# The last plain product of w_out by seven of its own, with one set of left sums and eight PSUM banks

## The chip, the cores and the metric

The kernel runs on one core of a Trainium2 chip. Times are microseconds on the device; lower is better. The core's engines are TensorE (PE: matmuls, and PEld: the loads of their stationary operand), VectorE (DVE), ScalarE (ACT), GpSimd (POOL) and SyncE (SP, which here only issues DMA). Each has its own queue of instructions and takes them in order; they meet at semaphores.

## The reference: what is computed

Normalised attention, and then a layer of two matmuls with silu between them; all in float32.

```python
q_n, k_n = rmsnorm(q, g_q), rmsnorm(k, g_k)            # q, k, v: (8, 12, 448, 64)
attn = softmax(q_n @ k_n.T / sqrt(64))
x = (attn @ v) as (3584, 768)                          # heads side by side
h = x @ w_in                                           # w_in: (768, 2048)
out = (h * sigmoid(h)) @ w_out                         # w_out: (2048, 768)
```

The change concerns the last line alone: a product of 3584x2048 by 2048x768.

## The kernel before

Attention for eight batches, `x @ w_in` and the silu come first; the silu's result goes to `hidden` in DRAM, transposed, so that rows of the 2048 lie on the partitions. They end near 904 us. The rest of the time is the second matmul, and all that follows here is about it.

**Quads.** The 3584 rows of the output are cut into 7 quads of 512. `quad(q)` computes one: a left operand of 512x2048 (from `hidden`) by the right operand `w_out`, 2048x768, which stays in SBUF. Each quad cuts both operands into 2x2 halves and forms the result from 7 products of sums of halves, in place of 8 (Strassen's scheme in Winograd's form). The products are numbered 1 to 7 and come in the order 4, 1, 2, 5, 6, 7, 3. Each is 256x1024 by 1024x384. The left sums of this outer level are four steps, `sum_left(0)` to `sum_left(3)`, each two VectorE operations of 1024 columns. They overwrite the halves in place, between the products that still need the old and those that need the new contents.

**Two ways to make a product.** `single` (L1063) does it plainly: for each of two tiles of 128 rows, 8 matmuls of 384 columns into one PSUM bank. A float32 matmul is two records in the trace, so a plain product is 32 records. `deep` (L1027) applies the scheme of seven once more inside the product: 7 small products of 4 matmuls of 192 columns, 56 records, in the order 1, 2, 6, 5, 3, 7, 4. Small product 1 takes a11, 2 takes a12, 4 takes a22, all raw quarters of the left operand; 6 takes the left sum s2, 5 takes s1, 3 takes s4, 7 takes s3. `sum_deep_left(name)` makes these four sums on VectorE, 512 columns each, in places `deep_lefts`; there are two sets of them, taken in turn by the products in `DEEP`. The sums of the right operand, `sum_deep_right(name)`, are made once, in the first quad, and kept for all quads in `deep_rights`: 16 VectorE operations of 192 columns for each product. One of every four overwrites part of w_out's half (b12), which the plain form of that same product still reads; so it comes after it.

**Evictions.** Each small product's bank is read once: 1 and 5 by a ScalarE copy (L1047, L1051) to p1 and p5, the others by a VectorE addition (`plus`, L704) that combines them. A product that adds to what is already in its result (`more`) has four additional additions of 192 columns. After product 7, eight VectorE operations of 384 columns combine the outer results, and `save_out` stores them.

**Which is deep.** Product 1 (`SINGLE`) is plain in every quad; its result goes to two places by ScalarE. In the first quad products 4, 2, 5 and 6 are plain too, since their right sums are made then, and 7 and 3 are deep. In the other quads all but 1 are deep.

**Order.** Everything is written out by hand in the order of issue. The left sums of a product are issued one or two products ahead of it, behind the evictions of an earlier product and ahead of those of the one before it. `fetch` (L966) loads the next quad's halves of the left operand, 1 MB each, from `hidden` as soon as the old contents have been used; it and most stores wait in SyncE's one queue.

**Banks.** PSUM has eight banks. Here two belong to the pool `ps_mm` (used by `single`) and six to `ps_alone` (used by `deep`). `bank(n)` (L726), which takes three of four tiles from `ps_alone` and one from `ps_mm` in turn, serves only the matmul before, `x @ w_in`.

Of the kernel before, what the change touches and what calls it, by code (L numbers as in the profile page):

```python
# [11 lines left out]
F32 = mybir.dt.float32  # L12
# [15 lines left out]
BANK = 512  # L28
# [152 lines left out]
def kernel(  # L181
# [25 lines left out]
    nc = tc.nc  # L207
# [75 lines left out]

    room = Room(nc, const, w_in, z)
    rms = [const.tile([P, 32], F32, name=f"rms{i}") for i in range(2)]
    spare = const.tile([P, 2 * J * D], F32, name="squares")
    minus_half = const.tile([P, 1], F32, name="minus_half")
    ident = const.tile([P, P], F32, name="ident")
    ones = const.tile([P, 3, D // 2], F32, name="ones")
# [4 lines left out]
    norm = Norm(nc, z, rms, minus_half)  # L294

    first_q = room.rest[:, ds(7 * nq, nq)]
    first_squares = [spare, room.rest[:, ds(6 * nq, nq // 2)]]
    g1, both = (
        room.rest[0:1, ds(room.rest.shape[1] - (i + 1) * 2 * D, 2 * D)].rearrange(
            "p (two d) -> p two d", two=2  # L300
# [156 lines left out]
def bounded(  # L457
# [41 lines left out]
    rows_q = [place["q0"], extra[:, 0:nq]]  # L499
    raw_q = [extra[:, ds(nq, nq)], extra[:, ds(2 * nq, nq)]]  # L500
    other = extra[:, ds(3 * nq, 4 * S)].rearrange("p (i h s) -> p i h s", i=2, h=2)
    scratch = [spare, extra[:, ds(3 * nq + 4 * S, nq // 2)]]


    n = 2 * room.COLS
# [194 lines left out]
    def minus(a, b, out):  # L700
        nc.vector.tensor_tensor(out=out, in0=a, in1=b, op=ALU.subtract)

    def plus(a, b, out):
        nc.vector.tensor_tensor(out=out, in0=a, in1=b, op=ALU.add)  # L704
# [11 lines left out]
    def right_sums(b11, b12, b21, b22, t1, t2, t4):  # L716

        minus(b12, b11, t1)
        minus(b22, t1, t2)
        minus(b22, b12, b12)  # L720
        minus(b21, t2, t4)
# [4 lines left out]
    def bank(n):  # L726
        turn = turns["next"] = (turns["next"] + 1) % 4
        if ps_alone is None or turn == 0:
            return ps_mm.tile([P, BANK], F32, name="mm")[:, 0:n]
        return ps_alone.tile([P, BANK], F32, name="alone")[:, 0:n]  # L730
# [210 lines left out]
    def take(n, *which):  # L941

        for i in which or range(len(regions)):
            a, at = regions[i]
            if at + n <= a.shape[1]:
                regions[i][1] += n
                return a[:, ds(at, n)]
        raise AssertionError

    SINGLE = 1  # L950
    DEEP = (4, 2, 5, 6, 7, 3)
    size = HF * 2 * P
    left = {at: take(size, 0) for at in ((1, 1), (0, 0), (0, 1))}
    left[1, 0] = take(size, 1)

    deep_lefts = [[take(size // 4, 8, 7, 6) for _ in range(4)] for _ in range(2)]
    results = {(1, 1): [take(z.HALF, i) for i in (7, 5)]}
    copies = [take(QUARTER, i) for i in (0, 0, 1, 2)]
    for at in ((1, 2), (2, 1), (2, 2)):
        a = take(2 * z.HALF)  # L960
        results[at] = [a[:, ts(t, z.HALF)] for t in range(2)]
    a = take(2 * z.HALF)
    aside = [a[:, ts(t, z.HALF)] for t in range(2)]
    deep_rights = {name: [take(4 * QUARTER) for _ in range(3)] for name in DEEP}

    def fetch(q, i, r):  # L966

        if q >= QUADS:
            return
        dst = left[i, r].rearrange("p (f c) -> p f c", f=HF)  # L970
        source = hidden.rearrange("(f r) p c -> r p f c", r=2)
        nc.sync.dma_start(dst, source[r, :, :, ds((4 * q + 2 * i) * P, 2 * P)])
# [7 lines left out]
    def sum_left(step):  # L980
        a11, a12, a21, a22 = (
            left[at].rearrange("p (n c) -> p n c", n=2) for at in ((0, 0), (0, 1), (1, 0), (1, 1))
        )
        for n in range(2):
            left_sums(a11[:, n], a12[:, n], a21[:, n], a22[:, n], a22[:, n], a11[:, n], a12[:, n], (step,))
# [5 lines left out]
    def deep_left(name):  # L991

        a = LEFTS[name].rearrange("p (i m t c) -> p m t i c", i=4, m=2, t=2)
        sums = [
            x.rearrange("p (i c) -> p i c", i=4) for x in deep_lefts[DEEP.index(name) % 2]
        ]
        return [a[:, 0, 0], a[:, 1, 0], a[:, 0, 1], a[:, 1, 1]] + sums

    def sum_deep_left(name):
        a11, a12, a21, a22, s1, s2, s3, s4 = deep_left(name)  # L1000
        plus(a21, a22, s1)
        minus(s1, a11, s2)
        minus(a11, a21, s3)
        minus(a12, s2, s4)

    def deep_right(name, i):
        b = right_one(name, i)
        h = [ts(k, QUARTER) for k in range(2)]
        return [b[:, 0, h[0]], b[:, 0, h[1]], b[:, 1, h[0]], b[:, 1, h[1]]] + [
            x[:, ts(i, QUARTER)] for x in deep_rights[name]  # L1010
        ]

    def sum_deep_right(name):

        for i in ORDER:
            right_sums(*deep_right(name, i))

    def of_seven(name, a, b):

# [4 lines left out]
            5: (s1, t1), 6: (s2, t2), 7: (s3, b12),  # L1024
        }[name]

    def deep(name, out, more, then=lambda t, h: None):  # L1027

        a = deep_left(name)
        out = [[x[:, ts(h, QUARTER)] for h in range(2)] for x in out]  # L1030
        p1, u2, u3, p5 = copies

        def product(of):
            t = ps_alone.tile([P, BANK], F32, name="alone")[:, 0:QUARTER]
            for i in ORDER:
                x, y = of_seven(of, a, deep_right(name, i))
                nc.tensor.matmul(t, x[:, i], y, start=i == ORDER[0], stop=i == ORDER[-1])  # L1037
            return t

        def added(x, o):  # L1040

            if not more:
                return x
            plus(o, x, o)
            return o

        nc.scalar.copy(p1, product(1))  # L1047
        plus(product(2), added(p1, out[0][0]), out[0][0])
        then(0, 0)
        plus(product(6), p1, u2)  # L1050
        nc.scalar.copy(p5, product(5))  # L1051
        plus(u2, p5, u3)
        x = added(u3, out[0][1])
        plus(product(3), x, out[0][1])
        then(0, 1)
        plus(product(7), u2, u3)
        x = added(u3, out[1][0])
        plus(product(4), x, out[1][0])
        plus(u3, added(p5, out[1][1]), out[1][1])
        then(1, 0)  # L1060
        then(1, 1)

    def single(name, t):  # L1063

        a = LEFTS[name].rearrange("p (f t c) -> p f t c", f=HF, t=2)
        o = ps_mm.tile([P, BANK], F32, name="mm")[:, 0 : z.HALF]
        steps = [(i, m) for i in ORDER for m in range(2)]
        for n, (i, m) in enumerate(steps):
            nc.tensor.matmul(  # L1069
                o, a[:, 2 * i + m, t], right_one(name, i)[:, m],  # L1070
                start=n == 0, stop=n == len(steps) - 1,
            )
        return o

    def save_out(q, i, j):
        for t in range(2):
            store(
                nc, out, z, (4 * q + 2 * (i - 1) + t) * P, results[i, j][t], (j - 1) * z.HALF,
                nc.gpsimd if q == QUADS - 1 and i == 2 else nc.sync,
            )  # L1080

    def quad(q):
        c = results

        def product(name, out, more):
            if q > 0 or name in DEEP[4:]:
                deep(name, out, more)
                return
            for t in range(2):
                o = single(name, t)  # L1090
                if more:
                    plus(o, out[t], out[t])
                else:
                    nc.scalar.copy(out[t], o)
            sum_deep_right(name)

        if q == 0:
            fetch(0, 1, 0)
            sum_deep_right(7)
        product(4, c[2, 1], False)  # L1100
        sum_left(0)
        sum_left(2)
        if q == 0:
            sum_deep_right(3)
        else:
            sum_deep_left(2)
        for t in range(2):
            o = single(SINGLE, t)
            nc.scalar.copy(c[1, 1][t], o)
            nc.scalar.copy(c[1, 2][t], o)  # L1110
        sum_left(1)
        if q > 0:
            sum_deep_left(5)
        product(2, c[1, 1], True)
        save_out(q, 1, 1)
        sum_left(3)
        if q > 0:
            sum_deep_left(6)
        product(5, c[2, 2], False)
        fetch(q + 1, 1, 1)  # L1120
        sum_deep_left(7)
        product(6, c[1, 2], True)
        fetch(q + 1, 0, 0)
        sum_deep_left(3)
        product(7, aside, False)
        for t in range(2):
            plus(aside[t], c[1, 2][t], aside[t])
            plus(c[1, 2][t], c[2, 2][t], c[1, 2][t])
            plus(c[2, 2][t], aside[t], c[2, 2][t])
            plus(c[2, 1][t], aside[t], c[2, 1][t])  # L1130
        save_out(q, 2, 2)
        save_out(q, 2, 1)
        fetch(q + 1, 1, 0)
        if q == QUADS - 1:

            def then(t, h):
                store(
                    nc, out, z, (4 * q + t) * P, c[1, 2][t][:, ts(h, QUARTER)],
                    z.HALF + h * QUARTER, *((nc.scalar, nc.sync)[:: 1 if h else -1]),
                )  # L1140

            deep(3, c[1, 2], True, then)
            return
        sum_deep_left(4)
        product(3, c[1, 2], True)
        save_out(q, 1, 2)
        fetch(q + 1, 0, 1)
# [406 lines left out]
```

## Time and profile before

| | |
|---|---|
| time, median of 3 runs | 1371.86 us (1369.43 to 1373.31) |
| span of the profiled execution | 1369.6 us |
| second matmul (first to last TensorE record) | 903.7 to 1363.0 us |
| `deep`'s matmuls, L1037, busy | 346.94 us in 2128 records |
| `single`'s matmuls, L1069, busy | 114.66 us in 352 records |
| mean granted TensorE clock | 0.995 |

The page gives busy time by engine; a chain of waits follows the execution back from its last instruction; the windows give busy time by engine in a stretch; the timeline gives the instructions of a stretch in order, "x2" being two of a kind merged, with the idle time ahead of one and what ended it in brackets. A name such as `work`, `rows`, `x`, `sums_x`, `stage`, `parts`, `squares` or `W` in a line is the big SBUF tile in which a piece lies, since the second matmul reuses the first part's room; `mm` and `alone` are the two PSUM pools.

### The profile page before, as it was taken

To read this page: it belongs to the slowest core of one execution; us is meant where nothing else is said; L and a number is where in the kernel's file an instruction comes from. 1 tells how busy PE (TensorE), PEld (TensorE's weight loads), DVE (VectorE), ACT (ScalarE), POOL (GpSimd) and SP (SyncE) were. 2 spreads that over 40 slices of the span, in tenths; PEclk is the share of its full clock that TensorE was granted. 3 is DMA by queue.
4 is the path that set the end of the run, shared out by engine and by line. 5 is a ranking of instruction groups with operands and counts; after the bars stand their busy time and mean duration, and the time that the engine had idled before them with its cause. 6 is when DMAs were issued, how large, how long until landed. Compare 5 with 4: busy or idle time off the path is not lost.

```text
span 1369.6 us, 19386 instructions
## 1 busy us (share of the span) xinstructions
PE 1335.0 (97%) x7185; PEld 818.4 (60%) x7185; DVE 886.6 (65%) x1497; ACT 517.5 (38%) x882; POOL 342.5 (25%) x241
## 2 busy tenths in 40 slices
PE   7998999999999999999999999999999999999998
PEld 4333444444444444444444455556898989898987
DVE  3887867785644444744443586677877676777775
ACT  5875555655455545544644244320000010100000
POOL 4764444343332332233221044410000000000001
PEclk9999999999999999999999999999999999999999
DMA  7663445333223222322221257422323232322311
GB/s 176 190 160 101 111 133 152 93 103 80 78 74 96 78 73 77 104 78 78 78 79 37 99 167 252 157 96 64 105 74 97 73 97 79 97 91 85 113 58 38
DMA packets 175404, 139.40 MB, mean 102 GB/s; under 512 B 104036, under 2 KB 159268, under 8 KB 175300
## 3 DMA queue, kind: packets, MB, share of 16 engines
q1 hardware_dynamic: 174624, 137.08, 34.1%
q8 instruction: 59, 0.97, 0.3%
q0 software_dynamic: 352, 0.79, 0.2%
q14 instruction: 45, 0.37, 0.1%
q10 hardware_dynamic: 324, 0.20, 0.1%
HBM read 88.47 MB, written 41.29 MB: 95 GB/s over the span
## 4 chain that ended last, share of the span: by engine, by line
PE 90%; DVE 4%; ACT 2%; issue 2%; SPq 1%; DMA 1%; DVEq 0%; ACTq 0%
PE mm L745 28%; PE alone L1037 25%; PE av L611 9%; PE mm L1069 8%; PE sc L579 8%; PE alone L745 7%; PE sc L546 1%; PE sc L561 1%; PE sc L645 1%; DVE work L654 1%; PE mm L645 1%; ACT work L584 1%; DVE work L625 1%; DVE rms L396 1%; DMA hidden<-stage 0%
## 5 line engine op out<-in xcount | busy, mean ns | idle before, releaser
L745 PE MATMUL mm<-x,W 128*128 128x448 f32 x636 | 255.5, 546 | 5.2 <-DVE stage L704 2.7
L584 ACT ACTIVATE work<-sc,rms 128x448 f32<-128x448 f32 x324 | 184.1, 631 | 88.4 <-PE sc L579 74.9
L424 POOL TENSOR_TENSOR rms<-rms,minus_half 128x14 f32<-128x14 f32 (+4 forms) x55 | 138.5, 2520 | 251.8 <-DVE rms L420 199.9
L745 PEld LDWEIGHTS mm<-x,W 128*128 128x128 f32 x636 | 118.3, 191 | 127.7 <-issue 107.1
L745 PE MATMUL mm<-sums_x,W 128*128 128x448 f32 x456 | 183.0, 542 | 0.8 <-DVE parts L704 0.8
L579 PE MATMUL sc<-work 64*64 64x448 f32 x1344 | 165.0, 548 | 6.1 <-ACT work L584 4.0
L625 DVE TENSOR_TENSOR work<-work 128x896 f32<-128x896 f32 (+1 forms) x114 | 124.9, 1130 | 58.8 <-ACT work L584 56.6
L611 PE MATMUL av<-work,rows 64*64 64x448 f32 x1296 | 153.7, 548 | 7.8 <-issue 2.8
L745 PEld LDWEIGHTS mm<-sums_x,W 128*128 128x128 f32 x456 | 85.3, 190 | 86.5 <-issue 81.1
L451 POOL DMA_DIRECT2D out_dram<-x x4 | 2.2, 565 | 450.6 <-DVE x L704 450.6
L611 PEld LDWEIGHTS av<-work,rows 64*64 64x64 f32 x1296 | 51.9, 133 | 96.5 <-issue 86.8
L579 PEld LDWEIGHTS sc<-work 64*64 64x64 f32 x1344 | 52.2, 133 | 88.4 <-issue 34.7
L1037 PE MATMUL alone<-W,rows 128*128 128x192 f32 x552 | 103.1, 326 | 0.0
L396 DVE TENSOR_REDUCE rms<-squares 112x8 f32<-112x512 f32 (+1 forms) x80 | 52.4, 655 | 73.0 <-ACT squares L395 72.2
L1037 PEld LDWEIGHTS alone<-W,rows 128*128 128x128 f32 x552 | 92.0, 190 | 0.0
L1069 PE MATMUL mm<-W,work 128*128 128x384 f32 x264 | 88.7, 486 | 0.0
L1037 PE MATMUL alone<-W,work 128*128 128x192 f32 x468 | 88.1, 326 | 0.0
L760 POOL TENSOR_TENSOR parts<-parts,stage 128x448 f32<-128x448 f32 x31 | 42.1, 1357 | 163.7 <-DVE parts L704 163.5
L1037 PEld LDWEIGHTS alone<-W,work 128*128 128x128 f32 x468 | 78.1, 190 | 0.0
L1047 ACT COPY work<-alone 128x192 f32<-128x192 f32 x38 | 12.1, 318 | 165.2 <-PE alone L1037 138.1
L1069 PEld LDWEIGHTS mm<-W,work 128*128 128x128 f32 x264 | 50.2, 190 | 35.0
L878 ACT ACTIVATE stage<-stage 128x896 f32<-128x896 f32 x63 | 57.3, 945 | 26.1 <-DVE stage L704 25.3
(192 smaller groups left out, 1960.0 us busy)
## 6 DMA issues: line engine op xcount, KB each, us to landing
hidden<-stage SPq DMA_DIRECT2D x63, 448.0 KB, 2.8
work<-hidden SPq DMA_DIRECT2D x21, 1024.0 KB, 5.4
rows<-in_moe_w_out_dram SPq DMA_DIRECT2D x32, 384.0 KB, 3.3
W<-in_moe_w_in_dram SPq DMA_DIRECT2D x22, 512.0 KB, 4.8
rows<-in_k_dram SPq DMA_DIRECT2D x48, 192.0 KB, 3.0
work<-work SPq DMA_DIRECT2D x144, 56.0 KB, 1.9
rows<-in_q_dram SPq DMA_DIRECT2D x36, 224.0 KB, 3.6
x<-hidden SPq DMA_DIRECT2D x7, 1024.0 KB, 5.8
```

Source lines behind the costliest of these rows:

```text
L396: nc.vector.tensor_reduce(out=out, in_=t.rearrange("p (n d) -> p n d", n=n), axis=AX.X, op=ALU.add)
L424: nc.gpsimd.tensor_tensor(out=t, in0=t, in1=half, op=ALU.pow)
L579: nc.tensor.matmul(two[ds(half * D, D), h, 0:S], keys[rows, ts(half, D)], qT[rows, pair, :], start=True, stop=True,)
L584: nc.scalar.activation(eleft[:, h] if j == LEFT else weights(c, j)[:, i, h], two[:, h, 0:S], AF.Exp, scale=norm.column(c, i, h, j),)
L611: nc.tensor.matmul(sums[i][ds(h * D, D), :], v, w, start=(j == 0 and step == 1), stop=(j == LEFT - 1 and step == 1),)
L625: nc.vector.tensor_tensor(out=total, in0=total, in1=more, op=ALU.add)
L645: nc.tensor.matmul(t[ds(h * D + i * n, n), :], ones[:, which + i if which else 0], eleft[:, h] if which else w()[:, i, h], start=(k == 0), ...
L745: nc.tensor.matmul(t, self.left(name, s), self.right(name, s), start=s == ends[0], stop=s == ends[1])
L760: nc.gpsimd.tensor_tensor(out=u2, in0=u2, in1=p5, op=ALU.add)
L878: nc.scalar.activation(t, t, AF.Silu)
L1037: nc.tensor.matmul(t, x[:, i], y, start=i == ORDER[0], stop=i == ORDER[-1])
L1069: nc.tensor.matmul(o, a[:, 2 * i + m, t], right_one(name, i)[:, m], start=n == 0, stop=n == len(steps) - 1,)
```

## The change

It makes product 1 deep as well, in all quads but the first, so that all seven products of a quad are products by seven of their own; and in the first quad product 6 becomes deep in place of plain. For the additional right sums (one more product, three pieces of 768 columns) it needs room in SBUF. It gets it by keeping one set of left sums in place of two: the sums of the next product (`following`) are now made inside `deep`, step by step, as the current product's small products leave their places free. The tile `squares` grows by 256 columns, and pieces move between the big tiles. `deep` and `single` both take their banks from `bank`, over all eight in turn. In the first quad the right sums are made in another order, and those of product 5 are put off in four pieces (`owed`), one inside each of the next four deep products. At the end of `deep` the result out[1][1] is now finished before small product 4 is evicted.

```diff
-    spare = const.tile([P, 2 * J * D], F32, name="squares")
+    spare = const.tile([P, 3 * J * D], F32, name="squares")
...
-    SINGLE = 1
-    DEEP = (4, 2, 5, 6, 7, 3)
+    DEEP = (4, 1, 2, 5, 6, 7, 3)
+    FIRST = DEEP.index(6)
...
-    deep_lefts = [[take(size // 4, 8, 7, 6) for _ in range(4)] for _ in range(2)]
-    results = {(1, 1): [take(z.HALF, i) for i in (7, 5)]}
-    copies = [take(QUARTER, i) for i in (0, 0, 1, 2)]
+    deep_lefts = [take(size // 4, 8, 6) for _ in range(4)]
+    results = {(1, 1): [take(z.HALF, i) for i in (0, 5)]}
+    copies = [take(QUARTER, i) for i in (8, 1, 2, 6)]
...
-    deep_rights = {name: [take(4 * QUARTER) for _ in range(3)] for name in DEEP}
+    deep_rights = {
+        name: [take(4 * QUARTER, 3, 4, 6, 1, 2, 7, 5) for _ in range(3)]
+        for name in (7, 3, 4, 6, 2, 5, 1)
+    }
...
-    def deep(name, out, more, then=lambda t, h: None):
+    def deep(name, out, more, following, then=lambda t, h: None):
...
-            t = ps_alone.tile([P, BANK], F32, name="alone")[:, 0:QUARTER]
+            t = bank(QUARTER)
...
         nc.scalar.copy(p5, product(5))
         plus(u2, p5, u3)
         x = added(u3, out[0][1])
+        if owed:
+            owed.pop(0)()
         plus(product(3), x, out[0][1])
         then(0, 1)
+        sum_deep_left(following, (0, 1))
         plus(product(7), u2, u3)
         x = added(u3, out[1][0])
+        plus(u3, added(p5, out[1][1]), out[1][1])
+        then(1, 1)
+        sum_deep_left(following, (2,))
         plus(product(4), x, out[1][0])
-        plus(u3, added(p5, out[1][1]), out[1][1])
         then(1, 0)
-        then(1, 1)
+        sum_deep_left(following, (3,))
...
-        o = ps_mm.tile([P, BANK], F32, name="mm")[:, 0 : z.HALF]
+        o = bank(z.HALF)
...
-            if q > 0 or name in DEEP[4:]:
-                deep(name, out, more)
+            n = DEEP.index(name)
+            if q > 0 or n >= FIRST:
+                deep(name, out, more, DEEP[(n + 1) % len(DEEP)])
                 return
...
-        if q == 0:
+        first = q == 0
+        if first:
             fetch(0, 1, 0)
             sum_deep_right(7)
         product(4, c[2, 1], False)
+        if first:
+            sum_deep_right(4)
         sum_left(0)
         sum_left(2)
-        if q == 0:
+        if first:
             sum_deep_right(3)
-        else:
-            sum_deep_left(2)
+        product(1, c[1, 1], False)
         for t in range(2):
-            o = single(SINGLE, t)
-            nc.scalar.copy(c[1, 1][t], o)
-            nc.scalar.copy(c[1, 2][t], o)
+            nc.scalar.copy(c[1, 2][t], c[1, 1][t])
         sum_left(1)
-        if q > 0:
-            sum_deep_left(5)
+        if first:
+            sum_deep_right(6)
+            sum_deep_right(1)
         product(2, c[1, 1], True)
         save_out(q, 1, 1)
+        if first:
+            sum_deep_left(6)
+            sum_deep_right(2)
         sum_left(3)
-        if q > 0:
-            sum_deep_left(6)
         product(5, c[2, 2], False)
+        if first:
+            owed.extend(lambda i=i: sum_deep_right(5, (i,)) for i in ORDER)
         fetch(q + 1, 1, 1)
-        sum_deep_left(7)
         product(6, c[1, 2], True)
         fetch(q + 1, 0, 0)
-        sum_deep_left(3)
         product(7, aside, False)
...
-        sum_deep_left(4)
         product(3, c[1, 2], True)
```

## The prediction, made before the changed kernel ran

> **What bounds the kernel now.** I read the busy shares of the page first, then the chain of waits over the last 370 us, then busy time quad by quad, then VectorE's own timeline.
>
> ```profile
> PE 1335.0 (97%) x7185; PEld 818.4 (60%) x7185; DVE 886.6 (65%) x1497; ACT 517.5 (38%) x882; POOL 342.5 (25%) x241
> ```
>
> ```profile
> 903.66 51.60 PE mm L1069 x160
> 955.26 27.30 PE alone L1037 x168
> 982.56 10.32 PE mm L1069 x32
> 992.88 54.60 PE alone L1037 x336
> ...
> 1307.16 10.32 PE mm L1069 x32
> 1317.48 45.51 PE alone L1037 x280
> 1362.99 0.02 issue
> 1363.02 0.63 DVE work L704 x2
> ```
>
> This is the second linear layer. Columns: start, length, what. The chain is nothing but TensorE from 903.66 to 1362.99, without one gap: TensorE is the bound here, and only its number of columns or a new wait can move the end. L1069 is the plain product of halves (`single`), L1037 the product by seven of its own (`deep`). The first quad has five plain products (51.60 us, so 10.32 each), then three deep (27.30, so 9.10 each; the third is the next quad's first). In each later quad product 1 alone is plain.
>
> ```profile
> 982.56:1047.48 64.92, 64.92 (x369) 60.68 (x369) 46.31 (x94) 5.54 (x16) 0.00 (x0) 1.00 0.30 93
> 1242.24:1307.16 64.92, 64.92 (x369) 60.68 (x369) 46.31 (x94) 5.54 (x16) 0.00 (x0) 1.00 0.29 89
> ```
>
> One row is a quad from plain product to plain product: length, then TensorE, weight load, VectorE, ScalarE, GpSimd. TensorE is full, VectorE busy 46.31 of 64.92 us (71%), ScalarE 9%. VectorE is the engine that the change loads more.
>
> ```profile
> 920.17 2.35 DVE L704 TENSOR_TENSOR work<-x,work 128x1024 f32<-128x1024 f32 x2
> 922.44 2.35 DVE L701 TENSOR_TENSOR x<-work,x 128x1024 f32<-128x1024 f32 x2
> 924.71 0.35 DVE L701 TENSOR_TENSOR stage<-x 128x192 f32<-128x192 f32 x1
> ...
> 929.50 2.35 DVE L701 TENSOR_TENSOR work<-work 128x1024 f32<-128x1024 f32 x2
> ...
> 994.06 0.68 DVE L704 TENSOR_TENSOR squares<-work 128x512 f32<-128x512 f32 x1
> ...
> 995.39 0.68 DVE L701 TENSOR_TENSOR rows<-work 128x512 f32<-128x512 f32 x1
> ...
> 996.59 0.35 DVE L704 TENSOR_TENSOR parts<-parts,work 128x192 f32<-128x192 f32 x1
> ```
>
> Starts, not durations, give what VectorE spends, since neighbours overlap: an outer left sum (`sum_left`, one step) 2.27 us; the right sums of one product (16 operations, 924.71 to 929.50) 4.79 us; the four left sums of a deep product 2.53 us, the first two of them 1.33 us.
>
> **What the Trainium skill says.** "VectorE: DVE Perf Modes", section on the TRN2 errata, prices an fp32 two-tensor addition at (N+151)/0.96 ns: 357 for 192 columns, 691 for 512. The groups here read 355 to 358 and 683 to 692, so it agrees. "TensorE: Matmul & The Clock Gate", section "Wait — 56ns, not 53.3ns?", gives a warm matmul N/2.4 GHz plus about 2.5 ns: 82.5 for 192 columns. The chain has 9.10/56 = 162.5 ns a record, which is twice the 80 plus 2.5; and 10.32/32 = 322.5, twice 160 plus 2.5. So the columns cost the same in both forms, and a deep product gains one eighth of them, less 24 records' fixed 2.5 ns. The same page, section on the array, says VectorE is a strict FIFO: an operation that waits holds all behind it. "PSUM — Partial Sum Buffer", specifications, has 8 banks in all; two pools of 2 and 6 tiles of a bank are all eight.
>
> **The change part by part.**
>
> *Seven products become deep.* Product 1 in quads 1 to 6 and product 6 in the first quad (the first four names, 4, 1, 2, 5, stay plain there). Each saves 10.32 - 9.10 = 1.22 us of TensorE: 7 x 1.22 = 8.54 us, all on the chain. First quad: plain from 903.66 to 944.94, then 6, 7, 3 deep to 972.24.
>
> *VectorE's additional work in a quad:* four left sums 2.53 us and seven operations of 192 columns on product 1's results, about 2.3 us. 46.3 + 4.8 = 51.1 of 63.70 us, 80%. It stays below the bound; the two copies to c[1,2] go on on ScalarE.
>
> *One set of left sums.* This is the risk. s1 and s2 of the following product are now made behind the eviction of this product's 3 (its fifth), s4 behind that of 7, s3 behind that of 4. Overwriting waits for nothing: 5 and 6, the readers of s1 and s2, are done before 3. TensorE's next reader is the following product's third, 6, which starts 2.60 us (2 x 1.30) after that product. Evictions start 0.21 us after TensorE has gone to the next small product. I count from T, where product 4 starts, with VectorE caught up; products then start at T+9.1, +18.2, ...:
> - 4 to 1: 3 is ready at 6.71, evicted 7.0, sums 8.35. Needed 11.70.
> - 1 to 2: the tail of 4 ends at 10.65 (s3); two outer sums 4.54 make 15.2; four operations up to the eviction of 3, 1.5, and 1.33 make 18.0. Needed 20.8: 2.8 us spare.
> - 2 to 5: `sum_left(1)` ends near 22.8; 3 of product 2 is ready at 24.9; sums 26.6, needed 29.9.
> - 5 to 6 after `sum_left(3)`: 35.7, needed 39.0.
> - 3 to the next quad's 4: after product 7's tail come the eight combinations, 4.24 us (they run from 965.81 to 970.05 now), so they end 5.8 after product 3's start; six operations 1.97 + 0.3, sums 1.33: 9.4 of 11.7 us.
> So all hidden, with 2.3 us at the tightest. s4 and s3 are needed 2.6 and 3.9 us later than s2 and have more.
>
> *First quad.* VectorE has the right sums too. Those of 7 move out of `stage`, so the wait of 3.16 us for `hidden<-stage` (911.50) goes; they end near 912. Then: 4 (waits for its product, 913.98) 918.3; outer 0 and 2, 922.9; 3, 927.7; outer 1, 930.0; right sums of 6 and 1, 939.6; two evictions of product 2, 940.6; left sums of 6, 943.1 (needed 947.5); right sums of 2, 947.9; outer 3, 950.2. Behind these queue the evictions of deep 6, from 950.2: 1.7 for four, an owed quarter of 5's right sums 1.2, eviction 0.3, sums for 7 at 954.8. TensorE wants them at 944.94 + 9.10 + 2.60 = 956.6: 1.8 us spare. At the end of this quad (combinations to 969.0, four operations, an owed quarter, sums) 973.5 against 974.8: 1.3 spare, the least of all.
>
> *Eight banks.* A bank is needed again eight small products later, 10.4 us, in place of six (7.8 us). With evictions at most 6.7 us behind the start of their product, no bank is waited for.
>
> *Fetches.* The fetch of (0,1) sits in SyncE's queue behind the stores of product 3, as now; I expect its issue some 4 us into the new quad and, from 5.1 us to landing, the data at 9 us; wanted at 17. Hidden.
>
> *The tail.* In the last quad the combinations start 0.95 us later, since s4 and s3 of product 3 are now made inside product 7. ScalarE issues the store of the first quarter ahead of its copy of p5, so VectorE's chain behind that comes later too; evicting 4 last gives part of it back. I take +0.5 us (between -0.3 and +1.0).
>
> Sum: -8.54 + 0.5 = -8.0; 1371.86 - 8.0 = 1363.8 us.
>
> **Rivals.**
> - *First quad late.* If the sums of 7 and of the next 4 come 1 to 2.5 us beyond their spare time (say because the right sums still start at 911.5), TensorE loses 2 to 5 us once: 1366 to 1369, take 1367. For it: the spare 1.3 and 1.8 us. Against: VectorE waits for product 4 at 913.98 anyway, which swallows most of that delay.
> - *Gain eaten.* One handover a quad 0.7 us late (six times, 4.2 us) and 4 us in the first quad: 1363.8 + 8.2 = 1372. For it: VectorE is a FIFO and goes to 80%. Against: it would take 3 us of error in a count whose parts are measured.
> - *Slower.* Three handovers a quad each 1 us late: 18 us, 1382. Against: the same, three times over; it needs a wait that I don't see, such as a left sum held by a load.
>
> **How the numbers follow.** Forecast 0.80, first quad late 0.09, gain eaten 0.05, slower 0.06. The three times before spread 3.9 us, so the forecast alone carries about 2 us either way. Range: 1360.8 (full gain, tail no dearer, a fast median) to 1367.6, which takes in most of the first rival; the other two, 1 in 10, are left out. 0.3% is 4.1 us, so faster means below 1367.7: the forecast and most of the first rival, 0.88; same 0.06; slower 0.06.
>
> **What would show it.** In the new chain of waits: four plain products (41.3 us) from about 903.7 and then L1037 alone to the end, some 410 us, without a gap; quads of 63.70 us; VectorE near 51 us in each. Wrong would be: weight loads or matmuls of L1037 that wait for VectorE's L701 or L704 at the third small product of a deep one (sums late), for evictions at its start (banks), or VectorE waiting for a `hidden` load. A quad at 63.7 us with an end not 8 us earlier would put the error in the first quad or the tail.

## The result and the profile after

The changed kernel takes 1364.08 us (median of 4 runs, 1360.00 to 1364.99) against 1370.64 us for the kernel before in the same runs (1369.03 to 1373.31). The ratio is 0.9944, 95% interval 0.9918 to 0.9971: faster by about 0.6%. The prediction was 1363.8 us. That it lies within 0.3 us is in part luck: it took 8.0 us off a median of 1371.86, where the kernel before has 1370.64 beside the changed one. The change itself is -7.7 us by the ratio and -6.6 us by the medians.

The page's line of TensorE, and the chain of waits of the changed kernel over the second matmul (start, length, what). `deep`'s matmuls are now L1047, `single`'s L1084; `alone` and `mm` alternate since all take their banks from both pools.

```profile
PE 1325.9 (97%) x7353; PEld 838.3 (62%) x7353; DVE 918.5 (67%) x1592; ACT 517.6 (38%) x884; POOL 342.7 (25%) x241
```

```profile
904.46 10.32 PE alone L1084 x32
914.78 5.16 PE mm L1084 x16
919.94 15.48 PE alone L1084 x48
935.42 5.16 PE mm L1084 x16
940.58 5.16 PE alone L1084 x16
945.74 2.60 PE alone L1047 x16
948.34 1.30 PE mm L1047 x8
949.64 3.90 PE alone L1047 x24
...
1339.64 3.91 PE alone L1047 x24
1343.58 0.36 DVE x L704
```

Four plain products, 41.28 us, and from 945.74 on deep ones alone: each piece begins where the last one ends. 904.46 + 41.28 + 45 x 9.10 = 1355.24 us, where TensorE's last record ends too. The chain is drawn over to VectorE at 1343.58 because VectorE is what ends last, in the last 12 us; TensorE goes on without a gap beside it. The same sum for the kernel before ended at 1362.99, with a start 0.80 us earlier: the stage is 8.55 us shorter. The later start is not read as an effect of the change; in the profiles of the edited kernels below the stage starts anywhere between 903.3 and 905.5.

Two stretches of the changed kernel, each as long as a quad; length, then busy time of TensorE, weight load, VectorE, ScalarE, GpSimd:

```profile
1036.35:1100.05 63.70, 63.70 (x394) 63.70 (x393) 50.13 (x106) 5.39 (x16) 0.00 (x0) 1.00 0.30 90
1100.05:1163.75 63.70, 63.70 (x394) 63.70 (x393) 50.13 (x106) 5.39 (x16) 0.00 (x0) 1.00 0.30 93
```

VectorE went from 46.3 of 64.92 us to 50.1 of 63.70, 79%, and no weight load waited in these quads.

How near it is to waiting can be read from VectorE's timeline. First the end of the first quad, then that of the third, each with TensorE's first matmul record that reads the new s2 in its own fence (these weights are the piece of `rows` that VectorE has just written):

```profile
973.23 0.68 DVE L704 TENSOR_TENSOR squares<-work 128x512 f32<-128x512 f32 x1
973.95 0.69 DVE L701 TENSOR_TENSOR rows<-squares,work 128x512 f32<-128x512 f32 x1
...
1099.06 0.68 DVE L704 TENSOR_TENSOR squares<-work 128x512 f32<-128x512 f32 x1
1099.78 0.69 DVE L701 TENSOR_TENSOR rows<-squares,work 128x512 f32<-128x512 f32 x1
```

```profile
975.48 1.46 PE L1047 MATMUL alone<-rows 128*128 128x192 f32 x8
...
1102.88 1.46 PE L1047 MATMUL alone<-rows 128*128 128x192 f32 x8
```

s2 is ready at 974.64 for a matmul at 975.48: 0.84 us to spare. In the later quad it is ready at 1100.47 for 1102.88: 2.41 us. The prediction had 1.3 and 2.3. The weight load, which is what takes s2 in, starts 0.16 us ahead of its matmul (at 975.32 and 1102.72), so strictly the spare time is 0.68 and 2.25 us.

### The profile page after: what moved, and what is told of

Read it like the earlier page. It is cut to its first block, busy times and chain, and to the rows that moved or that the text cites. A ratio compares the mean times of both kernels' runs of the same rounds, so it can differ in the third digit from the quotient of the medians.

```text
span 1362.3 us, 19801 instructions
## 1 busy us (share of the span) xinstructions
PE 1325.9 (97%) x7353; PEld 838.3 (62%) x7353; DVE 918.5 (67%) x1592; ACT 517.6 (38%) x884; POOL 342.7 (25%) x241
## 4 chain that ended last, share of the span: by engine, by line
PE 89%; DVE 5%; issue 3%; ACT 2%; SPq 1%; DMA 0%; POOL 0%; ACTq 0%; DVEq 0%; POOLq 0%
PE mm L745 29%; PE alone L1047 22%; PE av L611 8%; PE sc L579 8%; PE mm L1047 7%; PE alone L745 7%; PE alone L1084 2%; PE sc L546 1%; PE sc L561 1%; PE sc L645 1%; PE mm L645 1%; PE mm L1084 1%; DVE work L654 1%; ACT work L584 1%; DVE work L625 1%
## 5 line engine op out<-in xcount | busy, mean ns | idle before, releaser
L1047 PE MATMUL alone<-W,rows 128*128 128x192 f32 x488 | 92.0, 326 | 0.0
L1047 PEld LDWEIGHTS alone<-W,rows 128*128 128x128 f32 x488 | 81.4, 190 | 0.0
L1047 PE MATMUL alone<-W,work 128*128 128x192 f32 x382 | 72.2, 326 | 0.0
L1047 PEld LDWEIGHTS alone<-W,work 128*128 128x128 f32 x382 | 63.8, 190 | 0.0
L654 DVE RECIPROCAL work<-sc 128x224 f32<-128x224 f32 x36 | 55.7, 1548 | 11.1 <-PE sc L645 11.1
L1057 ACT COPY squares<-alone 128x192 f32<-128x192 f32 x34 | 10.8, 318 | 136.9 <-PE alone L1047 78.4
L395 ACT ACTIVATE squares<-rows 128x512 f32<-128x512 f32 (+1 forms) x74 | 44.7, 605 | 47.1 <-DVE rms L396 46.3
```

Source lines behind the costliest of these rows:

```text
L395: nc.scalar.activation(t, rows, AF.Square)
L654: nc.vector.reciprocal(out=r[0][:, rows], in_=t[:, rows])
```

## The experiments

All edits are made to the changed kernel. Ratios are to the kernel before, measured in the same runs; the changed kernel's is 0.9944. "Stage" is the time from the first to the last start of a matmul record of the second matmul in the profile: 449.5 us in the changed kernel. A quad is named by its place, the first to the seventh; "quads 1 to 6" in the texts on record are the second to the seventh.

### Product 1 plain again

```diff
-                deep(name, out, more, DEEP[(n + 1) % len(DEEP)])
+                deep(name, out, more, None if name == 4 else DEEP[(n + 1) % len(DEEP)])
...
-        product(1, c[1, 1], False)
+        else:
+            sum_deep_left(2)
         for t in range(2):
-            nc.scalar.copy(c[1, 2][t], c[1, 1][t])
+            o = single(1, t)
+            nc.scalar.copy(c[1, 1][t], o)
+            nc.scalar.copy(c[1, 2][t], o)
```

> Product 1 plain again in quads 1 to 6, all else as changed (one set of left sums; those of product 2 made ahead of product 1 instead of inside product 4). Theory (columns of TensorE are all of the gain): quads go from 63.70 back to 64.92 us, six times 1.22 = 7.3 us more than the changed kernel, about 1371.4 us, no gap in TensorE's chain. Rival (part of the gain comes from the new order of evictions or the eight banks): under 5 us more.

Product 1 is plain in every quad again. In the second to the seventh it reads its half of w_out after the right sums have overwritten a part of it; the work is the same. 1369.41 us, ratio 0.9996 (0.9986 to 1.0006): 0.52 percentage points over the changed kernel, 7.1 us. The stage takes 456.8 us, 7.3 more, and its chain shows the plain product every 64.92 us:

```profile
1112.34 10.32 PE alone L1084 x32
...
1177.26 10.32 PE alone L1084 x32
```

So six of the seven conversions account for 7.1 us of the gain, 1.2 us each, with the new order and the eight banks left in.

### Fewer banks

```diff
-            t = bank(QUARTER)
+            t = ps_alone.tile([P, BANK], F32, name="alone")[:, 0:QUARTER]
```

with the pool's 6 banks, then with 4 and 3 (`bufs` of `ps_alone`).

> Deep products take their banks from the pool of six alone; the plain ones of the first quad still from all eight. Theory (no bank is ever waited for: VectorE starts a product's evictions at most 6.7 us after it, a bank of six comes round after 7.8): no change, 1364 us within 2, no gap in the chain. Rival (the single set of sums puts evictions later, and the additional banks are what absorbs that): gaps at the second or third small product of product 2 and of the next quad's 4, 0.5 us or more each, 6 us or more in all.

> Deep products take turns over four banks. Theory (a bank is waited for only if small product 2 is evicted later than the start of the fourth small product after it): in the changed kernel's second quad VectorE ends that eviction 6.1 us after the start of product 1 and 6.2 us after that of 3, and with four banks it must be out by 6.5: no change, 1364 within 2. Rival (more banks take up unevenness that this does not see): gaps in products 1 and 3, 3 us or more in all.

> The same with three banks: small product 2 must be out by 5.2 us. Theory: products 1 and 3 wait 0.9 and 1.0 us, the other five (3.0 to 4.6 us) do not: about 2 us a quad, +13 us, about 1377, and the waits are at the fifth small product (3) of those two products. Rival (banks are not bound to evictions in this way): no change, or waits everywhere.

Six banks: 1363.19 us, ratio 0.9944 (0.9927 to 0.9960). Four: 1363.12 us, 0.9944 (0.9927 to 0.9960). Neither has a matmul record that waits in this stage, which takes 449.5 us in both. Three: 1374.01 us, 1.0018 (1.0011 to 1.0025), the stage 459.6 us. So a bank was waited for only with three, and products 1 and 3 are the ones that wait, once each in a quad, as expected. But the wait is another than I named, and with 0.75 us of the weight load it is shorter than the 0.9 and 1.0 us expected. TensorE, ScalarE and VectorE in product 1 of the third quad, with three banks (brackets: idle before, and what ended it):

```profile
1052.29 0.32 ACT L1061 COPY rows<-alone 128x192 f32<-128x192 f32 x1 [3.58 <-PE alone L1047]
1052.66 0.30 PEld L1047 LDWEIGHTS alone<-x,rows 128*128 128x128 f32 x2 [0.75 <-ACT rows L1061]
1052.66 0.59 PE L1047 MATMUL alone<-x,rows 128*128 128x192 f32 x2 [0.45 <-ACT rows L1061]
1052.71 0.35 DVE L704 TENSOR_TENSOR work<-alone,squares 128x192 f32<-128x192 f32 x1
```

The fifth small product starts 0.05 us after ScalarE's copy of p5 and before VectorE begins the eviction of the second. It took the bank that the fourth had just left, for the other two were not yet read; the pool doesn't hand its banks out in strict turns. The count "needed again so many small products later" was therefore not what holds, though its verdict for eight, six and four banks was right.

### The sums behind the last eviction

```diff
-        sum_deep_left(following, (0, 1))
...
-        sum_deep_left(following, (2,))
...
-        sum_deep_left(following, (3,))
+        sum_deep_left(following)
```

> The four left sums of the following product all behind the eviction of small product 4, same work. Theory (hidden because of their place; from the trace of the changed kernel the sums end 3.5 us ahead of need, but 3.1 at 1 to 2 and 2.6 at 3 to 4, and the move costs 2.7 to 3.6): TensorE waits about 1.0 us at 3 to 4 and 0.2 at 1 to 2, quads of about 65 us, and about 1 us more in the first quad, +8 us (range 5 to 11), about 1372. Rival (only VectorE's total counts, 50.1 of 63.7 us a quad, which this does not alter): no change, quads of 63.70.

1374.27 us, ratio 1.0026 (1.0010 to 1.0041), 0.82 points or 11 us over the changed kernel: the whole gain gone, with the same operations. The stage takes 458.8 us, 9.3 more; the rest lies behind it. The matmuls that waited at the start of the third and the fifth quad, always the third small product of product 4, and then a weight load of product 2 in the second quad:

```profile
1042.34 1.57 PE L1047 MATMUL alone<-rows 128*128 128x192 f32 x8 [0.87 <-DVE rows L701]
...
1172.37 1.57 PE L1047 MATMUL mm<-rows 128*128 128x192 f32 x8 [0.87 <-DVE rows L701]
```

```profile
995.70 1.27 PEld L1047 LDWEIGHTS alone<-sums_x,rows 128*128 128x128 f32 x8 [0.20 <-issue]
```

VectorE's total is not what decides; the place of the sums is. The hand-over from 3 to 4 is the one that breaks, as expected. The small wait expected from 1 to 2 came too, 0.20 us in every second quad; it shows on the weight load alone, and no matmul record waited there.

### More work for VectorE: one, two and three additional operations

```diff
-        sum_deep_left(following, (0, 1))
+        sum_deep_left(following, (0, 0, 0, 0, 1))     # three more; (0, 0, 1) one, (0, 0, 0, 1) two
```

> s1 is computed four times over ahead of s2: three additional operations of 512 columns a product, 0.61 us each, 1.8 us a product, 12.8 us a quad. Theory (spare time at each handover): at 3 to 4 the delay of two products adds up, 9.1 + 3.6 = 12.7 against 11.7 us: 1.0 late; at 1 to 2 17.7 + 3.6 = 21.3 against 20.8: 0.5 late; quads of about 65.2 us, first quad 3 us, +12 us, about 1376. Rival (total): VectorE at 50.1 + 12.8 = 62.9 of 63.7 us still fits, no change.

> s1 computed twice over ahead of s2: one additional operation a product, 0.72 us as the repeated one took in the run with three. Theory (spare time): at 3 to 4 9.13 + 1.44 = 10.6 of 11.7 us, at 1 to 2 17.7 + 1.4 = 19.1 of 20.8: quads stay at 63.70 us although VectorE goes from 50.1 to 55.2; only the end of the first quad, with 1.0 us spare, is some 0.4 us late: +0.4 us, no change that can be told. Rival (TensorE and VectorE hold each other up as soon as VectorE has more, as the +41 us with three suggests, so each additional operation costs a third of that): +10 us or more.

> s1 computed three times over: two additional operations a product, 1.45 us at the 0.72 us that a repeated one took. VectorE then has 50.1 + 10.2 = 60.3 of 63.70 us a quad. Theory (spare time at the handovers): at 3 to 4 9.13 + 2.90 = 12.0 against 11.7 us, 0.3 late and some 0.3 more for the weight load that waits with it; at 1 to 2 17.7 + 2.9 = 20.6 of 20.8, just in time; 4 us over six quads and 2 us at the end of the first quad: +6 us, about 1369.5. Rival (VectorE's total): it fits, no change.

| additional operations a product | time, us | ratio (interval) | stage, us |
|---|---|---|---|
| 0 (the changed kernel) | 1364.08 | 0.9944 (0.9918 to 0.9971) | 449.5 |
| 1 | 1364.85 | 0.9956 (0.9941 to 0.9970) | 450.3 |
| 2 | 1374.79 | 1.0023 (1.0011 to 1.0035) | 459.9 |
| 3 | 1404.59 | 1.0256 (1.0238 to 1.0274) | 487.8 |

With three, the miss is large: +41 us where I had 12. A repeated s1 took 0.72 us from start to start, not 0.61, so VectorE was busy 64.3 us a quad, more than the 63.7 there were. But a quad took 69.5 us. In the third, weight loads waited at four hand-overs, those to products 4, 2, 5 and 6, for 2.13, 1.58, 1.21 and 0.89 us: 5.8 in all, which is what the quad grew by. VectorE in its turn stood idle for 5.2 us. Neither theory had that size, so this run does not separate them. The other two do. With one more, VectorE is busy 54.8 us a quad, quads stay at 63.70 us, and TensorE waits once in the whole stage, at the end of the first quad, for 0.59 us: 0.84 to spare less two delays of 0.72 is 0.60 late.

```profile
975.78 1.54 PE L1047 MATMUL alone<-rows 128*128 128x192 f32 x8 [0.59 <-DVE rows L701]
```

With two more, VectorE is still at 58.1 of 63.7 us, but each quad is 65.1 us long. These are waits of TensorE in its third quad and at the start of the fourth:

```profile
1043.97 1.57 PE L1047 MATMUL alone<-rows 128*128 128x192 f32 x8 [0.38 <-DVE rows L701]
1071.84 1.54 PE L1047 MATMUL alone<-sums_x,rows 128*128 128x192 f32 x8 [0.21 <-DVE rows L701]
...
1109.08 1.54 PE L1047 MATMUL alone<-rows 128*128 128x192 f32 x8 [0.47 <-DVE rows L701]
```

2.41 to spare less 2.90 is 0.49 late, and 0.38 to 0.47 is what is seen. The size of +11 us (6 expected) is more than the gaps: a quad grows by 1.4 us for 0.4 to 0.6 us of gaps on TensorE. The late operand is the stationary one, and its weight load is late by more than its matmul: 0.67 to 0.74 us at product 4. Smaller waits of weight loads follow, in the third quad at products 5 and 6 (0.48, 0.16), in the fourth at 2, 5 and 6 (0.18, 0.35, 0.28), most of them with no gap on TensorE. With product 4's they come to 1.3 and 1.6 us, which is the 1.4 us a quad. With 2.30 us at the end of the first quad (2 expected) the weight loads waited 10.7 us in the whole stage, and the stage is 10.4 us longer. So the forecast was right for the hand-over from 3 to 4 and left out those behind it.

### The store behind the copy of p5

```diff
         plus(product(2), added(p1, out[0][0]), out[0][0])
-        then(0, 0)
         plus(product(6), p1, u2)
         nc.scalar.copy(p5, product(5))
+        then(0, 0)
```

> Last product of all: ScalarE's copy of p5 ahead of the store of the first quarter in its queue. Theory (the store held the copy, the copy VectorE's chain): p5 is there when wanted, VectorE's last operation ends 0.4 to 0.7 us earlier after TensorE's last, and the span's end after TensorE's last goes from 7.06 to about 6.5 us; -0.5 us, to be seen in the profile only. Rival (the last eviction waits for TensorE's last small product anyway, or the first quarter's store is now the late one): no difference, or later.

The last product of the changed kernel, timeline of ScalarE and VectorE:

```profile
1352.40 0.55 ACTq L451 DMA_DIRECT2D out_dram<-work  x1
...
1353.39 0.36 DVE L704 TENSOR_TENSOR sums_x<-x,rows 128x192 f32<-128x192 f32 x1 [0.77 <-ACT rows L1061]
...
1355.84 0.35 DVE L704 TENSOR_TENSOR work<-mm,work 128x192 f32<-128x192 f32 x1
```

and of the edited one:

```profile
1351.10 0.32 ACT L1060 COPY rows<-alone 128x192 f32<-128x192 f32 x1 [3.58 <-PE alone L1047]
...
1352.42 0.36 DVE L704 TENSOR_TENSOR sums_x<-x,rows 128x192 f32<-128x192 f32 x1
...
1354.99 0.35 DVE L704 TENSOR_TENSOR work<-mm,work 128x192 f32<-128x192 f32 x1
```

Without the store ahead of it the copy is done before VectorE wants it, and the wait of 0.77 us is gone. TensorE's last record ends at 1355.24 in the first and 1354.92 in the second: the last eviction follows it by 0.60 us there and 0.07 here, so 0.53 us is what the move is shown to save on VectorE. From TensorE's end to the span's end it was 7.06 us in the changed kernel and is 6.18 here, but that figure varies by itself: with the same tail it is 6.66 in the profile with six banks, 6.95 with four and 6.89 with one more operation. The time, 1362.86 us, ratio 0.9939 (0.9925 to 0.9954), is the lowest of all here, though it can't be told from the changed kernel's.

### The first quad's right sums on GpSimd

Products 1, 2 and 5 of the first quad stay plain because VectorE has the right sums to make just then, while GpSimd is idle. The edit, in part:

```diff
-    FIRST = DEEP.index(6)
+    FIRST = DEEP.index(1)
...
+            sum_deep_right(1)
+            sum_deep_left(1)
+            sum_deep_right(2)
+            for name in (5, 6, 7, 3):
+                gpsimd_right(name)        # the same four subtractions by nc.gpsimd.tensor_tensor
         product(4, c[2, 1], False)
+        if first:
+            gpsimd_right(4)
```

> First quad: products 1, 2 and 5 deep as well; the right sums of 5, 6, 7, 3 and 4 on GpSimd, which is idle here, those of 1 and 2 on VectorE. GpSimd's 448-column addition took 1.36 us, so about 0.6 us for 192 columns, some 10 us for a product's 16. Theory (what keeps these three plain is VectorE's time in the first quad alone): three more times 1.22 = 3.7 us less than the changed kernel, no gap, about 1360. Rival (GpSimd takes over 0.9 us for one, or slows VectorE beside it): TensorE waits in the first quad for right sums of 5 to 7, and the gain is eaten, 1364 or more.

> Both of the former. Theory: they are in different places and add up, -4.2 us, about 1359.5 us, 0.8% below the kernel before. Rival: as above for each.

In this kernel the first quad makes `sum_left(2)` after `sum_left(1)`, so s3 is taken from an overwritten a11; the work is the same. 1377.35 us, ratio 1.0045 (1.0032 to 1.0058), and with the store moved as well 1375.16 us, 1.0032 (1.0020 to 1.0044). The rival was right: in place of -3.7 us it cost 13. The moved store adds nothing here that can be told. VectorE beside the busy GpSimd:

```profile
908.63 0.35 DVE L701 TENSOR_TENSOR W<-x 128x192 f32<-128x192 f32 x1
909.02 0.64 DVE L701 TENSOR_TENSOR W<-x,W 128x192 f32<-128x192 f32 x1
909.58 0.74 DVE L701 TENSOR_TENSOR x<-x 128x192 f32<-128x192 f32 x1
910.24 0.74 DVE L701 TENSOR_TENSOR W<-x,W 128x192 f32<-128x192 f32 x1
...
936.57 0.34 DVE L704 TENSOR_TENSOR work<-alone,squares 128x192 f32<-128x192 f32 x1
936.84 0.34 DVE L704 TENSOR_TENSOR x<-alone,squares 128x192 f32<-128x192 f32 x1
```

An operation with both inputs in SBUF goes from 0.35 us to between 0.64 and 0.74; one that reads a PSUM bank (`alone`) stays at 0.34. The Trainium skill, "SBUF — State Buffer", section "SBUF: two separate sides", has a pair of ports that GpSimd and VectorE lock from each other, VectorE where it has two SBUF inputs and the GpSimd operation reads SBUF. This trace agrees in which operations are slowed. So in this stretch the operations lent to GpSimd slowed those left on VectorE. The left sums for products 1 and 2 came late, and TensorE waited 3.16 us at the one and 7.90 us at the other:

```profile
921.05 1.83 PE L1054 MATMUL alone<-W,rows 128*128 128x192 f32 x8 [3.16 <-issue]
939.97 2.93 PE L1054 MATMUL alone<-sums_x,rows 128*128 128x192 f32 x8 [7.90 <-DVE rows L701]
```

These two waits less the 3.7 us gained would make 7.4, not 13. Most of the rest lies right behind them: eight such records take 1.46 us elsewhere, and here the three small products from 921.05 on take 5.66 us and those from 939.97 on 6.98, in place of 3.90. The granted clock reads 0.66 over 921.05 to 926.00 and 0.50 over 939.97 to 946.00.

## Why the prediction was right, step by step

- **The total.** The mechanism is right and so is its size in the profile: -8.55 us in the stage. That the medians meet within 0.3 us is partly luck, as said above; the profiles alone give -7.3 us, with 0.80 of start and 0.44 of tail against the 8.55.
- **Seven products, 1.22 us each.** Right: 8.54 us predicted, 8.55 us shorter in the chain. `plain1` puts six of them back and has 7.1 us of the 7.3.
- **VectorE's additional work.** Predicted 51.1 us a quad, measured 50.1: 3.8 us more than before in place of 4.8. It lies beside TensorE; `one_more` adds 4.7 us a quad, and the quads stay at 63.70 us.
- **One set of left sums.** Right: no wait. The spare time at the tightest hand-over of a quad was 2.4 us (predicted 2.3), and `sums_last` and `two_more` show that it is used up where they say. That the hand-over and not VectorE's share is what decides is shown by `sums_last`, which loses the gain with no operation added, and by `two_more`, where VectorE with 58.1 of 63.7 us still had room.
- **First quad.** Right that it fits and where it is tightest: 0.84 us to spare, predicted 1.3, and `one_more` broke there first. A part of its working was wrong: I held the right sums of 4 until that product's end, as the half that they overwrite is still read; the profile has them start at 912.92, before that product's end at 914.78. By the kernel's order this is allowed, as the later of the two tiles reads the half chunk by chunk.
- **Eight banks.** The verdict (no wait, not needed) was right; the rule of turns it was drawn from was not.
- **Tail.** +0.5 us predicted, +0.44 measured (7.06 us from TensorE's end to the span's end, against 6.62), but not by the way that was named, and so by luck. The combinations do start later against TensorE's end, by 0.60 us (0.95 predicted). But VectorE's last operation ends 0.95 us behind TensorE's last record, and it was 1.04 us in the kernel before: VectorE's chain is not the later one. That the store stands ahead of the copy is true, but it did so before the change too, and VectorE's wait for the copy was longer there:

```profile
1360.83 0.36 DVE L704 TENSOR_TENSOR x<-work,sums_x 128x192 f32<-128x192 f32 x1 [1.05 <-ACT sums_x L1051]
```

The 0.44 us lies behind VectorE's end (6.11 us from there to the span's end, against 5.57), and it is about as large as the scatter of the same tail from profile to profile, 6.66 to 7.06 us. Whether the change made the tail longer stays open; `store_later` shows how VectorE's part of it can be shortened, not the cause of the 0.44.
- **Fetches.** Predicted hidden; no VectorE operation of the quads waits for a load, and no experiment delayed one.

What is left open: whether a second set of left sums in the new order would change anything was not tried, since there is no room for one beside seven sets of right sums; with no wait on the single set in the profile there is nothing for it to take away. Nor was product 6 of the first quad put back to plain by itself; its 1.22 us rests on the chain alone.

## What to carry to other kernels

When TensorE's chain has no gap, what a change in its columns does to the stage in the profile can be priced to the tenth of a microsecond (here 8.54 against 8.55); the whole time scatters by more. What needs care is the hand-over of operands that another engine makes just in time. Compute for each such hand-over when it is ready and when it is wanted, not the engine's share: here VectorE could be 79 to 86% busy with no loss in a quad, at 91% a gain of 8 us was gone, and with no more work at all but the sums issued last it was gone too. Read the spare time and the waits on the weight load where the operand handed over is the stationary one. And when an operand is reused across steps from one place, issue the sums as soon as the old reader is done, between evictions and not behind them.

## What the runs showed of the hardware that was not expected

- A wait costs more than the gap on TensorE's matmuls, and the idle time of its weight load is the better measure. With three banks, two gaps of 0.45 us a quad made it 1.44 us longer (the period of the fifth small product of product 1 is 65.14 us), and the weight load was idle 0.75 us each time. The same holds where the stationary operand is late: with the sums last, the gaps sum to 6.9 us, the idle times of weight loads to 9.2, and the stage is 9.3 us longer; with two more operations it is 5.2, 10.7 and 10.4.
- VectorE operations that write the same place again start 0.72 us apart for 512 columns, as s2 does behind s1, which it reads (973.23 and 973.95), against 0.60 to 0.61 for a pair that doesn't depend on one another.
- GpSimd's subtractions of 192 columns took 0.59 to 1.57 us beside VectorE, the longest beside VectorE's operations of 1024 columns.
- After a wait of 7.90 us TensorE's granted clock read 0.50 for the next 6 us, and eight records took 2.93 us in place of 1.46; after a wait of 2.04 us (two more operations, first quad) eight took 1.54.
